# Fetching the next expert's weights, and the gates for a range check, in twelve paced pieces in a fused GateLoop and mixture-of-experts kernel

## The chip, the cores and the metric

The kernel runs on one core of a Trainium2 chip. The metric is the device time of one execution in microseconds (us), as the median of several runs; lower is better. The core has a matrix engine (TensorE; PE in the profile), whose results land in PSUM, a vector engine (DVE), an activation engine (ACT), a general engine (GpSimd; POOL), and a queue engine (SP) that here only starts transfers between the chip's memory (HBM) and the on-chip memory (SBUF).

## The reference

Two blocks follow each other. The first is a gated linear recurrence over 768 steps for 4 x 8 heads of 48 elements: a complex gate `a` is limited in magnitude, multiplies a 48 x 48 state, the outer product of key and value is added, and the query reads the state. Its result, seen as 3,072 rows of 384, goes through a mixture of eight experts in which each row goes to the one expert with the largest logit:

```python
    mag = np.sqrt(a_re * a_re + a_im * a_im)
    scale = np.minimum(mag, 0.999) / (mag + 1e-06)
    a_re_n, a_im_n = (a_re * scale, a_im * scale)
    for t in range(S):
        ...
        S_re, S_im = (new_re + kv, new_im)
        y[:, :, t] = np.einsum('bhd,bhde->bhe', q[:, :, t], S_re)
...
    logits = x @ w_gate
    expert_idx = np.argmax(logits, axis=1)
...
        h = np.maximum(x_sorted[lo:hi] @ w1[e], 0.0)
        y_sorted[lo:hi] = h @ w2[e]
    y = y_sorted[inv_perm]
    return (gate_w[:, None] * y).astype(np.float32)
```

Everything is float32. Each expert has `w1` (384 x 1024) and `w2` (1024 x 384), 1.5 MB each.

## The kernel before, in words

**The first block** fills the time up to about 270 us. It works through the sequence in 24 chunks of 128 rows, in an order written out by priorities, and writes its rows to a buffer `xd` in HBM. Since the rows' logits are ready only at its end, the eight experts are then sorted by how many rows they have, and each takes a **place**: place 0 is the fullest. Each place has a fixed capacity (`CAPS`: 448, 416, 416, 408, 400, 384, 376, 360 rows), so its instructions don't depend on the data; only the expert's number does. That number is in the tile `owner`, and SP reads it into a register (`load_w`, L588) to address the weights.

**A place** is done by `expert` (L676) in two layers, on tiles that two places use in turn: `wa` (`w1`), `wb` (`w2`), `xg` (gathered rows), `xt` (those rows turned so that the 384 inputs lie on partitions), and `ht` (the hidden layer). Even places use one set of these tiles, odd places the other.

- *Hidden layer*: for each of the 8 columns `f` of 128 hidden units, three matmuls (`hps`, two recorded passes each, so 6 records) go into one of four PSUM buffers, and a relu takes the result to `ht`: VectorE for even `f`, ScalarE for odd `f`.
- *Output layer*: for each tile of 128 rows, eight matmuls (`yps`, 16 records) sum over `f`, VectorE multiplies by the row's gate, and GpSimd scatters the rows into the result (`scatter`, L657). Two PSUM buffers take turns. Capacities that aren't a multiple of 128 leave a small last tile: in places 1 to 4 it has 32, 32, 24 and 16 rows. Its eight matmuls go to four column strips of the array, ScalarE copies three partial sums (`z`), and VectorE adds them.

While place i runs, GpSimd gathers the rows of place i+1 with one indirect transfer for each 32 rows, between its scatters, and VectorE turns them (`turn`, L628) once the hidden layer of place i is evicted. Place 0 is different: its first two row tiles are done in the first block's tail (`early`), and the others at the start of this part.

**The weights** of place i+2 are requested after place i: `wa` in four transfers of 32 partitions (384 KB each) and `wb` in one of 1.5 MB. Since place i+2 uses place i's tiles, `wa` starts when place i's hidden layer has read them, and `wb` when its output layer has.

**The range check** looks at every gate `a`, in six parts (`in_range`, L919), because the first block uses a form that holds only in a range. For part j it fetches two tiles `rc` of 128 x 1536 (768 KB each, real and imaginary part; two buffers), and VectorE makes two passes with a compare and a sum. `verdict` (L934) reads the sums, adds them over the partitions with a small matmul (`bp`), and gives a flag. If it is set, a slow exact path is run after the experts; with these inputs it isn't, and only the test of the flag and the last scatter follow.

**Order.** A scheduler sets the order on each engine from the dependencies and the program's order, and adds the semaphore waits. An engine's instructions wait in that order. SP's queue in this part holds only the transfers of `wa`, `wb` and `rc`; those of `rc` have no dependency but their buffers, so the first five are queued ahead of place 1's weights. `T["mm"]` always holds the last matmul that was written.

Of the kernel before, what the change touches and what calls it, by code (L numbers as in the profile page):

```python
# [10 lines left out]
FP = mybir.dt.float32  # L11
# [6 lines left out]
SYNC = mybir.DependencyInfo(mybir.DependencyClass.Sync, mybir.DependencyReason.DATA)  # L18
NOSYNC = mybir.DependencyInfo(mybir.DependencyClass.NoSync, mybir.DependencyReason.DATA)

P = 128
# [17 lines left out]
def kernel(  # L39
# [12 lines left out]
    nc = tc.nc  # L52
# [4 lines left out]
    E, _, F = w1.shape  # L57
    KD, KF = DM // P, F // P
# [7 lines left out]
    T = {}  # L66

    def mm(o, lhsT, rhs, start=True, stop=True):
        T["mm"] = nc.tensor.matmul(o, lhsT=lhsT, rhs=rhs, start=start, stop=stop, skip_group_check=True)  # L69
        return T["mm"]  # L70
# [12 lines left out]
    def iota(pattern, name, base=0, cm=0):  # L83
# [16 lines left out]
        out=last, in_=ones, pattern=[[0, P]], base=-(P - 1), channel_multiplier=1, compare_op=OP.is_ge, fill=0.0  # L100
# [484 lines left out]
    def tiles(i):  # L585
        return -(-CAPS[i] // P)

    def load_w(i, after=None):  # L588
        o = own0 if i == 0 else owner[:, i : i + 1]
        ev = nc.sync.value_load(o[0:1, 0:1], min_val=0, max_val=E - 1)  # L590
        wa = EP[i % 2].tile([P, KD, F], FP, tag="wa", name="wa")
        parts = [(slice(0, P), w1[ds(ev, 1)].rearrange("o (k p) f -> p (o k) f", p=P))]
        if i >= SQ:
            w = w1[ds(ev, 1)].rearrange("o (a k j) f -> a j (o k) f", a=4, k=KD)
            parts = [(slice(a * Q4, (a + 1) * Q4), w[a]) for a in range(4)]
        for p, w in parts:
            ins = nc.sync.dma_start(out=wa[p], in_=w)
            if after is not None:
                tc.add_manual_dep(ins.ins, after.ins.name, SYNC, reason="rows first")
        wb = EP[i % 2].tile([P, KF, DM], FP, tag="wb", name="wb")  # L600
        nc.sync.dma_start(out=wb, in_=w2[ds(ev, 1)].rearrange("o (i p) d -> p (o i) d", p=P))
        T["w", i] = wa, wb

    def gather(i, t0, t1, rows=N):

# [22 lines left out]
    def turn(i, t0, t1, ps, end=None):  # L628

        xg = T["xg", i]  # L630
        if t0 == 0:
            T["xt", i] = EP[i % 2].tile([P, KD, CAPS[0]], FP, tag="xt", name="xt")
        c0, c1 = t0 * P, min(CAPS[i], t1 * P)
        if i >= SQ:
            j1 = -(-c1 // Q4)
            T["turned"] = nc.vector.transpose(
                out=T["xt", i][:, :, c0 : j1 * Q4].rearrange("p k (j s) -> p j k s", s=Q4),
                in_=xg[:, c0 // Q4 * (DM // 4) : j1 * (DM // 4)].rearrange("p (j k x) -> p j k x", x=Q4, k=KD),
            )
            behind(T["turned"], [T["held"]])  # L640
            return
        for d in range(KD):
            tp = ps.tile([P, 512], FP, tag="tp", name="tp")
            for t in range(t0, t1):
                n = min(P, CAPS[i] - t * P)
                ins = nc.tensor.transpose(
                    out=tp[:, (t - t0) * P : (t - t0) * P + n],
                    in_=xg[0:n, t * DM + d * P : t * DM + (d + 1) * P],
                    identity=ident[0:n, 0:n],
                )  # L650
                if end is not None:
                    behind(ins, [end])
            T["turned"] = (nc.scalar.copy if d % 2 else nc.vector.tensor_copy)(
                out=T["xt", i][:, d, c0:c1], in_=tp[:, 0 : c1 - c0]
            )

    def scatter(y, n, i, t, to=None):  # L657
        ins = nc.gpsimd.indirect_dma_start(  # L658
            out=out,
            out_offset=bass.IndirectOffsetOnAxis(ap=row[0:n, i, t : t + 1] if to is None else to[0:n], axis=0),  # L660
            in_=y[0:n],
            in_offset=None,
            bounds_check=N - 1,
            oob_is_err=False,
        )
        if "drained" in T:
            behind(ins, [T["drained"]])
        T["scattered"] = T["scattered", i, t] = ins
# [4 lines left out]
        behind(ins, [T["scattered"]])  # L673
        T["drained"] = ins

    def expert(i, t0, t1, psH, psO, yp, between=None):  # L676

        xt = T["xt", i]
        wa, wb = T["w", i]
        if t0 == 0:  # L680
            T["ht", i] = EP[i % 2].tile([P, KF, CAPS[0]], FP, tag="ht", name="ht")
        ht = T["ht", i]
        c0, c1 = t0 * P, min(CAPS[i], t1 * P)
        for f in range(KF):
            ps = psH.tile([P, 512], FP, tag="tp" if psH is psT else "h", name="hps")[:, 0 : c1 - c0]
            for d in range(KD):
                mm(ps, wa[:, d, f * P : (f + 1) * P], xt[:, d, c0:c1], d == 0, d == KD - 1)
            if f % 2:
                nc.scalar.activation(out=ht[:, f, c0:c1], in_=ps, func=AF.Relu)  # L689
            else:  # L690
                T["held"] = ts(out=ht[:, f, c0:c1], in0=ps, scalar1=0.0, scalar2=None, op0=OP.max)  # L691
        for t in range(t0, t1):
            if t == t1 - 2 and between is not None:
                between()
            n = min(P, CAPS[i] - t * P)
            if psO is psA:
                ps = psO.tile([P, DM], FP, tag="at", padded_shape=[P, 512], name="yps")
            else:
                T["left"] = T.get("left", sum(tiles(j) for j in range(E)) - EARLY) - 1
                po = psO if T["left"] % 2 else EP["last"]  # L700
                ps = po.tile([P, DM], FP, tag="y", padded_shape=[P, 512], name="yps")
            g = gate[0:n, i, t : t + 1]
            y = yp.tile([P, DM], FP, tag="y", name="y", bufs=2 if psO is psA else 10)
            hs = ht[:, :, t * P : t * P + n]
            if n > 64:
                for f in range(KF):
                    mm(ps[0:n], hs[:, f], wb[:, f], f == 0, f == KF - 1)
                if i == E - 1 and t == t1 - 1:
                    T["last"] = ps[0:n], g
                    return  # L710
                ts(out=y[0:n], in0=ps[0:n], scalar1=g, scalar2=None, op0=OP.mult)  # L711
            else:

                w = 32 if n <= 32 else 64
                parts = P // w
                for f in range(KF):
                    j = f % parts
                    mm(ps[j * w : j * w + n], hs[:, f], wb[:, f], f < parts, f >= KF - parts)
                z = yp.tile([P, DM], FP, tag="z", name="z")
                for j in range(1, parts):  # L720
                    nc.scalar.copy(out=z[j * w : j * w + n], in_=ps[j * w : j * w + n])  # L721
                tt(out=y[0:n], in0=ps[0:n], in1=z[w : w + n], op=OP.add)  # L722
                for j in range(2, parts):
                    tt(out=y[0:n], in0=y[0:n], in1=z[j * w : j * w + n], op=OP.add)  # L724
                ts(out=y[0:n], in0=y[0:n], scalar1=g, scalar2=None, op0=OP.mult)
            scatter(y, n, i, t)

    def early(t0, t1, end):

# [47 lines left out]
    for hp in range(HP):  # L777
        for i in range(2):
            nc.sync.dma_start(
                out=back[i * 64 : i * 64 + D, hp, DD:], in_=w_gate[hp * DD + i * D : hp * DD + (i + 1) * D, :]  # L780
# [84 lines left out]
    for g in range(NT):  # L865
        u, b = divmod(g, B)
# [42 lines left out]
    yp = pool2("yp", 2, reuse_waits="tile")  # L909
# [5 lines left out]
    NR_ = 6  # L915
    RW = N * DM // P // NR_
    inr = const([P, 2 * NR_], "inr")

    def in_range(j):  # L919
        a = [rp.tile([P, RW], FP, tag=f"rc{i}", name=f"rc{i}") for i in range(2)]  # L920
        for t, src in zip(a, (a_re, a_im)):
            s = src.rearrange("b h t d -> (b h t d)").rearrange("(p f) -> p f", p=P)
            nc.sync.dma_start(out=t, in_=s[:, j * RW : (j + 1) * RW])
        junk = rp.tile([P, RW], FP, tag="junk", name="junk", bufs=1)
        for i, (op, sc) in enumerate(((OP.max, A_MIN), (OP.mult, -1.0))):
            stt(
                out=junk, in0=a[1], scalar=sc, in1=a[0], op0=op, op1=OP.is_lt,
                accum_out=inr[:, 2 * j + i : 2 * j + i + 1],
            )
# [22 lines left out]
    for i in range(E):  # L952
        t0 = EARLY if i == 0 else 0
        if i == E - 1:
            verdict()
        if i + 1 < E:
            gather(i + 1, 0, tiles(i + 1))
        expert(i, t0, tiles(i), psH, psO, yp, (lambda: turn(i + 1, 0, tiles(i + 1), psG)) if i + 1 < E else None)
        if i in DRAINS:
            drain()  # L960
        if i + 2 < E:
            load_w(i + 2)
        if 1 <= i <= NR_:
            in_range(i - 1)

# [3 lines left out]
    with tc.If(nc.values_load(flag[0:1, 1:2], min_val=0, max_val=P * (NC + 1)) > 0):  # L969
# [135 lines left out]
        n, a = 1, 0  # L1105
# [145 lines left out]
```

## Time and profile before

| | |
|---|---|
| median of 3 runs | 563.99 us (560.99 to 564.17) |
| profiled execution | 561.03 us, of which the span is 559.3 us |
| TensorE busy | 523.6 us, 94% of the span |
| VectorE, ScalarE, GpSimd busy | 289.6, 214.3, 132.7 us |
| transfers | 73.5 MB, 131 GB/s over the span |
| granted TensorE clock, mean | 0.991 |

The places stand in the profile as follows (start of the hidden layer and of the output layer on PE, us):

| place | rows | hidden | output |
|---|---|---|---|
| 0 (tiles 2 and 3) | 192 | 298.49 | 308.83 |
| 1 | 416 | 316.81 | 333.68 |
| 2 | 416 | 350.68 | 369.75 |
| 3 | 408 | 386.75 | 405.71 |
| 4 | 400 | 422.70 | 443.19 |
| 5 | 384 | 460.18 | 477.39 |
| 6 | 376 | 492.87 | 508.03 |
| 7 | 360 | 523.65 | 538.25 |

In a line of the timeline the first number is the start in us from the span's start, the second the time to the end of the last of the merged instructions, then engine, line, operation, output and inputs, the shape, and how often; the bracket is the engine's idle time before it and what ended it. A matmul's end is modelled, not measured. A row of windows gives the window, its length, the busy time of PE, its weight loads, DVE, ACT and POOL with the number of instructions, the granted clock as a share of full speed, the busy share of the 16 DMA engines, and GB/s. In the page's second part each digit is the busy share of a fortieth of the span, in tenths.

### The profile page before, as it was taken

Reading aid. Unit: us, or ns where it says so; the run is one execution under the profiler, and the core shown is the slowest. Engines: PE = TensorE matmul, PEld = TensorE weight load, DVE = VectorE, ACT = ScalarE, POOL = GpSimd, SP = SyncE. Lnnn points to the kernel's source line nnn. Section 1 sums busy time; section 2 is a strip of 40 time slices with the busy share of each in tenths; the row PEclk is TensorE's granted clock in tenths of the full one; section 3 lists DMA queues with packets and bytes.
Section 4 is the critical chain, followed back from the end, with each engine's and each line's share of the span. In section 5 each row is a group of like instructions: output and inputs, shape, how many; then the busy total and the mean of one; then the engine's idle time right before and its main releaser. Section 6 shows DMA issues by size and latency. Waiting matters only on the chain. (4 is left out here: it accounts for less than half of the span.)

```text
span 559.3 us, 8295 instructions
## 1 busy us (share of the span) xinstructions
PE 523.6 (94%) x3154; PEld 370.8 (66%) x3154; DVE 289.6 (52%) x585; ACT 214.3 (38%) x323; POOL 132.7 (24%) x161
## 2 busy tenths in 40 slices
PE   3889979999999999999998999899899899999996
PEld 3666858878888898888766555455454455555663
DVE  5378687788789888785565221251442412212210
ACT  6877988876588874553200010111101102000000
POOL 3000000000000000001058555707347064370101
PEclk9989989999999999999999999999999899999999
DMA  9977691938655826503468966753865444650001
GB/s 164 187 102 103 112 142 22 180 60 168 116 86 115 150 55 140 74 30 139 174 222 222 265 196 137 252 133 73 307 142 189 144 112 148 135 171 18 26 2 41
DMA packets 167735, 73.49 MB, mean 131 GB/s; under 512 B 149053, under 2 KB 160343, under 8 KB 167688
## 3 DMA queue, kind: packets, MB, share of 16 engines
q1 hardware_dynamic: 162792, 63.12, 52.4%
q0 software_dynamic: 4896, 9.77, 5.9%
q8 instruction: 27, 0.44, 0.3%
q14 instruction: 20, 0.16, 0.1%
HBM read 63.34 MB, written 9.73 MB: 131 GB/s over the span
## 5 line engine op out<-in xcount | busy, mean ns | idle before, releaser
L69 PE MATMUL hps<-xt,wa 128*128 128x416 f32 (+7 forms) x432 | 136.8, 472 | 8.8 <-issue 4.2
L69 PE MATMUL yps<-wb,ht 128*128 128x384 f32 (+6 forms) x464 | 134.1, 487 | 0.0
L69 PEld LDWEIGHTS hps<-xt,wa 128*128 128x128 f32 x432 | 79.9, 192 | 62.7 <-issue 32.0
L616 POOL DMA_INDIRECT xg<-xd,tok x92 | 94.8, 1030 | 88.5 <-PE tp L332 40.6
L69 PEld LDWEIGHTS yps<-wb,ht 128*128 128x128 f32 (+6 forms) x464 | 75.1, 175 | 55.8 <-issue 8.6
L689 ACT ACTIVATE ht<-hps 128x416 f32<-128x416 f32 (+7 forms) x36 | 16.7, 467 | 151.7 <-PE hps L69 103.9
L711 DVE TENSOR_SCALAR y<-yps,gate 128x384 f32<-128x384 f32 (+1 forms) x23 | 14.2, 618 | 93.2 <-PE yps L69 76.5
L658 POOL DMA_INDIRECT out_dram<-y,row x28 | 29.2, 1044 | 118.6 <-DVE y L711 100.9
L69 PE MATMUL at<-qt,kt 96*128 96x128 f32 x384 | 53.9, 280 | 0.7 <-DVE am L340 0.7
L691 DVE TENSOR_SCALAR ht<-hps 128x416 f32<-128x416 f32 (+7 forms) x36 | 18.8, 527 | 68.6 <-PE hps L69 41.8
L261 POOL DMA_DIRECT2D ai<-cd x4 | 3.4, 839 | 211.0 <-ACT R L175 100.6
L69 PEld LDWEIGHTS at<-qt,kt 96*128 96x128 f32 x384 | 47.7, 192 | 4.5 <-issue 1.1
L69 PE MATMUL yt<-am,v 128*48 128x128 f32 x384 | 42.7, 281 | 0.6 <-DVE am L340 0.6
L340 DVE TENSOR_TENSOR am<-at,tri 128x512 f32<-128x512 f32 x48 | 33.0, 688 | 18.6 <-PE at L69 18.5
L721 ACT COPY z<-yps 32x384 f32<-32x384 f32 (+3 forms) x13 | 6.1, 470 | 84.2 <-PE hps L69 58.0
L69 PE MATMUL yt<-qt,G 96*48 96x128 f32 x320 | 35.7, 274 | 0.0
L332 PE MATMUL tp<-ident,K 128*96 128x128 f32 x192 | 33.5, 284 | 1.3 <-DVE K L323 1.1
L69 PEld LDWEIGHTS dk<-v,K 128*96 128x96 f32 x320 | 32.9, 168 | 2.1 <-issue 1.0
L69 PE MATMUL dk<-v,K 128*96 128x48 f32 x320 | 33.5, 244 | 0.2 <-DVE G L371 0.2
L332 PE MATMUL tp<-ident,Q 128*96 128x128 f32 x192 | 33.4, 277 | 0.0
L334 ACT COPY kt<-tp 96x512 f32<-96x512 f32 x48 | 27.9, 581 | 11.0 <-PE tp L332 10.8
L334 ACT COPY qt<-tp 96x512 f32<-96x512 f32 x48 | 28.2, 587 | 4.2 <-PE tp L332 4.2
(170 smaller groups left out, 667.2 us busy)
## 6 DMA issues: line engine op xcount, KB each, us to landing
wb<-in_moe_w_dram SPq DMA_DIRECT2D x8, 1536.0 KB
wa<-in_moe_w_dram SPq DMA_DIRECT2D x28, 384.0 KB
q<-in_q_dram SPq DMA_DIRECT2D x12, 384.0 KB
k<-in_k_dram SPq DMA_DIRECT2D x12, 384.0 KB
v<-in_v_dram SPq DMA_DIRECT2D x12, 384.0 KB
xd<-x SPq DMA_DIRECT2D x24, 192.0 KB
rc<-in_a_re_dram SPq DMA_DIRECT2D x6, 768.0 KB
rc<-in_a_im_dram SPq DMA_DIRECT2D x6, 768.0 KB
```

Of the source, the lines that this page charges most:

```text
L69: T["mm"] = nc.tensor.matmul(o, lhsT=lhsT, rhs=rhs, start=start, stop=stop, skip_group_check=True)
L261: nc.gpsimd.dma_start(out=T["ai", u][0:1, b0:b1].rearrange("p b h d -> p (b h d)"), in_=cd[1, u - 1 : u, b0 * DM : b1 * DM], accum_op=OP.add,)
L332: nc.tensor.transpose(out=tp[0:DD, j], in_=X[:, hg * 4 + j], identity=ident)
L334: nc.scalar.copy(out=t[0:DD], in_=tp[0:DD])
L340: tt(out=am, in0=at, in1=bc(tri, 1, 4), op=OP.mult)
L616: ins = nc.gpsimd.indirect_dma_start(out=T["xg", i][0:n, j * w : (j + 1) * w], out_offset=None, in_=view, in_offset=bass.IndirectOffsetOnA ...
L658: ins = nc.gpsimd.indirect_dma_start(out=out, out_offset=bass.IndirectOffsetOnAxis(ap=row[0:n, i, t : t + 1] if to is None else to[0:n], a ...
L689: nc.scalar.activation(out=ht[:, f, c0:c1], in_=ps, func=AF.Relu)
L691: T["held"] = ts(out=ht[:, f, c0:c1], in0=ps, scalar1=0.0, scalar2=None, op0=OP.max)
L711: ts(out=y[0:n], in0=ps[0:n], scalar1=g, scalar2=None, op0=OP.mult)
L721: nc.scalar.copy(out=z[j * w : j * w + n], in_=ps[j * w : j * w + n])
```

## The change

For places 2 to 7 the weights are no longer requested after place i-2. `load_w` returns a list of eight jobs, four for `wa` (as they were cut before) and four for `wb` (two columns `f` each, 384 KB). `load_range` makes four more: each of the two `rc` tiles in two halves of 384 KB. During place i (1 to 6) the twelve jobs are for place i+1's weights and for part i-1 of the range check: first the four of `wa`, then `wb` and `rc` in turn. `begin` starts the next job and makes it wait for the matmul written last. It is called after every second hidden column, in the middle of every full output tile, and after every scatter; what is left then is started at the place's end. `in_range` no longer fetches; it runs after its place, as before. Weights of places 0 and 1 are fetched as before.

```diff
     def load_w(i, after=None):
...
-        for p, w in parts:
-            ins = nc.sync.dma_start(out=wa[p], in_=w)
-            if after is not None:
-                tc.add_manual_dep(ins.ins, after.ins.name, SYNC, reason="rows first")
+        jobs = [(wa[p], w) for p, w in parts]
         wb = EP[i % 2].tile([P, KF, DM], FP, tag="wb", name="wb")
-        nc.sync.dma_start(out=wb, in_=w2[ds(ev, 1)].rearrange("o (i p) d -> p (o i) d", p=P))
+        w = w2[ds(ev, 1)].rearrange("o (i p) d -> p (o i) d", p=P)
         T["w", i] = wa, wb
+        if i < 2:
+            for n, (o, src) in enumerate(jobs + [(wb, w)]):
+                ins = nc.sync.dma_start(out=o, in_=src)
+                if after is not None and n < len(jobs):
+                    tc.add_manual_dep(ins.ins, after.ins.name, SYNC, reason="rows first")
+            return []
+        return jobs + [(wb[:, f : f + 2], w[:, f : f + 2]) for f in range(0, KF, 2)]
+
+    def begin(jobs):
+
+        if jobs:
+            o, src = jobs.pop(0)
+            ins = nc.sync.dma_start(out=o, in_=src)
+            tc.add_manual_dep(ins.ins, T["mm"].ins.name, SYNC, reason="pace")
...
-    def expert(i, t0, t1, psH, psO, yp, between=None):
+    def expert(i, t0, t1, psH, psO, yp, between=None, jobs=()):
...
                 T["held"] = ts(out=ht[:, f, c0:c1], in0=ps, scalar1=0.0, scalar2=None, op0=OP.max)
+            if f % 2:
+                begin(jobs)
...
                     mm(ps[0:n], hs[:, f], wb[:, f], f == 0, f == KF - 1)
+                    if f == KF // 2:
+                        begin(jobs)
...
             scatter(y, n, i, t)
+            begin(jobs)
...
+    def load_range(j):
+
+        T["rc"] = [rp.tile([P, RW], FP, tag=f"rc{i}", name=f"rc{i}") for i in range(2)]
+        jobs = []
+        for t, src in zip(T["rc"], (a_re, a_im)):
+            s = src.rearrange("b h t d -> (b h t d)").rearrange("(p f) -> p f", p=P)[:, j * RW : (j + 1) * RW]
+            jobs += [(t[:, c : c + RW // 2], s[:, c : c + RW // 2]) for c in (0, RW // 2)]
+        return jobs
+
     def in_range(j):
-        a = [rp.tile([P, RW], FP, tag=f"rc{i}", name=f"rc{i}") for i in range(2)]
-        for t, src in zip(a, (a_re, a_im)):
-            s = src.rearrange("b h t d -> (b h t d)").rearrange("(p f) -> p f", p=P)
-            nc.sync.dma_start(out=t, in_=s[:, j * RW : (j + 1) * RW])
+        a = T["rc"]
...
-        expert(i, t0, tiles(i), psH, psO, yp, (lambda: turn(i + 1, 0, tiles(i + 1), psG)) if i + 1 < E else None)
+        jobs = []
+        if 1 <= i <= NR_:
+            w = load_w(i + 1)
+            jobs += w[:4]
+            for x in zip(w[4:], load_range(i - 1)):
+                jobs += x
+        expert(i, t0, tiles(i), psH, psO, yp, (lambda: turn(i + 1, 0, tiles(i + 1), psG)) if i + 1 < E else None, jobs)
+        while jobs:
+            begin(jobs)
         if i in DRAINS:
             drain()
-        if i + 2 < E:
-            load_w(i + 2)
         if 1 <= i <= NR_:
             in_range(i - 1)
```

## The prediction

> **What bounds the kernel now.** I read the page's busy shares first, then the chain of waits, then the timeline of each engine over places 0 to 7 (290 us to the end), because only there does the change move anything.
>
> ```profile
> PE 523.6 (94%) x3154; PEld 370.8 (66%) x3154; DVE 289.6 (52%) x585; ACT 214.3 (38%) x323; POOL 132.7 (24%) x161
> ...
> DMA  9977691938655826503468966753865444650001
> ...
> PE 30%; issue 4%; another core or an unknown queue 1%; DMA 1%; ACT 1%; DVE 0%; POOLq 0%; ACTq 0%
> ...
> L926 DVE SCALAR_TENSOR_TENSOR junk<-rc,rc x12: 1715/1748/1759, 292.3 to 443.2; 128x1536 f32<-128x1536 f32 x12
> ```
>
> TensorE is busy 94% of the span, and the chain in the second half is its two layers, `hps` and `yps`. Transfers run in half to two thirds of the time there, in bursts. The fourth line (from the answer on tile `rc`) prices a range check: two passes of 1.75 us and 0.08 us for each accumulator read, 3.66 us of VectorE.
>
> What the change could win is PE idle time. From 290 us on the PE timeline has eleven gaps: 0.79, 0.41, 0.47, 0.26, 0.90, then 0.49, 1.18, 1.37, 0.51, 2.31, 1.35; 10.04 us in all. But not all of them are idle time of the array. PE, SP and PE again:
>
> ```profile
> 349.60 1.15 PE L69 MATMUL yps<-wb,ht 128*32 128x384 f32 x12
> 350.68 8.65 PE L69 MATMUL hps<-xt,wa 128*128 128x416 f32 x24
> 359.82 2.36 PE L69 MATMUL hps<-xt,wa 128*128 128x416 f32 x6 [0.49 <-DVE ht L691]
> 363.36 6.55 PE L69 MATMUL hps<-xt,wa 128*128 128x416 f32 x18 [1.18 <-issue]
> 369.75 2.42 PE L69 MATMUL yps<-wb,ht 128*128 128x384 f32 x7
> ...
> 353.50 0.39 SPq L601 DMA_DIRECT2D wb<-in_moe_w_dram  x1
> ...
> 422.70 10.34 PE L69 MATMUL hps<-xt,wa 128*128 128x400 f32 x30
> 435.35 8.01 PE L69 MATMUL hps<-xt,wa 128*128 128x400 f32 x18 [2.31 <-ACT ht L689]
> ```
>
> The last matmul of place 1's 32-row tile is recorded as over by 350.75, yet the `wb` transfer that waits for it starts at 353.50: the array finishes that tile 2.8 us after the record. From 353.50 to 369.75 are 16.25 us for 48 hidden matmuls; the undisturbed 48 of place 1 took 16.87 (316.81 to 333.68). So the array did not stand still, and the gaps at 359 and 362 only ate the lead of the records. Place 3 the same: 389.55 to 405.71, 16.16 us, against 16.87 x 408/416 = 16.55. Place 5: 462.33 to 477.39, 15.06 against 15.57. Only place 4 lost: 426.20 to 443.19 is 16.99 against 16.22, and against place 3 scaled (16.16 x 400/408 = 15.84) it is 1.1 us. So at most about 1.1 us of the last six gaps is real.
>
> **The change part by part.**
>
> *The range rows leave place 0.* Before, SP issues five of the twelve range transfers between 283.9 and 296, beside the row gathers of place 0. The gather of its last rows is issued at 284.38, and PE waits for it until 291.72 (0.79 us), with 0.41 more at 292.87 for a copy that came late with it. With that traffic gone the rows are there at 290.66; VectorE still has the eviction of 290.86 ahead of the copy, so the last transpose moves from 292.87 to about 292.0. Gain 0.9 us (ends 0 and 1.2). The four VectorE passes in place 0 go too; the 0.26 and 0.90 at 303.7 and 305.8 follow late relus while `wa` of place 1 is already flowing, which stays. I take 0 there, ends 0 and a gain of 1.2.
>
> *The burst after each place goes.* Before, place i+2's `wa` starts when place i's hidden layer is over, and `wb` with two or three range halves (3 MB) at place i's end. After, one piece of 384 KB starts at every second hidden column, in the middle and at the end of every output tile. Place 4's stall of 2.31 us came under that burst, and the clock after it was low. The columns are busy time of PE, PEld, DVE, ACT, POOL, then granted clock, DMA share, GB/s:
>
> ```profile
> 354.00:356.00 2.00, 2.00 (x7) 1.06 (x6) 1.00 (x2) 0.93 (x2) 1.39 (x3) 1.00 0.61 131
> 356.00:358.00 2.00, 2.00 (x7) 1.14 (x6) 0.09 (x1) 0.00 (x0) 1.69 (x2) 1.00 1.03 367
> ...
> 408.00:410.00 2.00, 2.00 (x8) 1.21 (x7) 1.97 (x3) 0.00 (x0) 0.00 (x0) 1.00 1.07 215
> ...
> 436.00:438.00 2.00, 2.00 (x4) 0.92 (x3) 0.19 (x1) 0.00 (x0) 0.00 (x0) 0.55 0.38 151
> ```
>
> Ends: the whole 1.1 us gained, or as much lost if the new pattern delays a place likewise. Three of the four like places lost nothing, so I take the gain of 1.1.
>
> *Are the weights in time?* `wa`'s four pieces start in the hidden layer and have the output layer's 17 us to land; `wb`'s last starts at the place's end and is first needed late in the next output layer's first tile, 17 us later. **A rule speaks against the change**: the Trainium skill, "DMA: Bandwidth & Descriptors", section "Bandwidth", wants transfers of 1 MiB or more, and the section "Anatomy of one DMA" fits, for transfers that GpSimd issues, a fixed 2.0 us plus bytes/436e9. By it a piece of 393,216 bytes takes 2.9 us, twelve in a row 35 us: as long as a place (36 us), so the next would wait for weights. The row at 408 us shows four such pieces, already cut so before, keeping the engines at share 1.07 and 215 GB/s with no gap between: 1.8 us each, the fixed part beside the piece ahead; and pieces over 128 partitions run at 367 to 404 GB/s, 1 us each. By the rows a place's twelve take 4 x 1.8 + 8 x 1.0 = 15 us of 34. I follow the rows: cost 0. If pieces did run one by one, the last would be late by a few us in each place.
>
> *The new wait: a range check behind its own last piece.* The last piece of `rc` always starts at the place's last matmul (T0). In places 1 to 4 `wb`'s last and it follow T0, in places 5 and 6 the last three. In the order that the program builds, VectorE then has: relu of column 0 of the next place, two adds for the small tile, **both passes of the check**, relus of columns 2, 4, 6 (in places 6 and 7 one pass after each of relus 0 and 2). Who waits: relu 2 stands behind the check, and matmuls of column 6 need its PSUM buffer (four). Landing: issues take 0.40 and 0.58 us (SP rows at 353.5), data flow about 2 us after the issue (131 GB/s in the first window, 367 in the next), 0.79 MB at 395 GB/s take 2.0: T0 + 4.5; with three pieces, T0 + 5.5. Column 6 starts at T0 + 6 x 2.05 = 12.3; relu 2 takes 0.6 and the check 3.66, so it must start by T0 + 8.0. Even with relu 0 as late as now (395.97, T0 + 6.4, in place 3) and 1.6 us of relu and adds behind it, it starts at T0 + 8.0. I take 0.2 us in all; below nothing isn't possible, as this wait is new; the upper end is the slow rival.
>
> *The verdict moves.* Its matmul `bp` stood ahead of place 7's hidden layer; now it stands behind 17 of its 24, and waits for the last check: T0 + 5.5, pass 1.83, relu 0.53, pass 1.83, relu 0.53, compare 0.17 = T0 + 10.4. The array gets there at T0 + 17/24 x 14.6 = 10.3. No margin: 0.5 us, ends 0 and 2.
>
> *Signals and waits.* Matmuls signal 14 times more and PE waits 13 times more, twice in the middle of each first output tile. Rows of `yps`, which already carry four waits there, show 0.0 idle: cost 0; at 0.05 us each, 0.7. SP has nothing else queued in these places, so its waits hold up nobody; gathers, scatters and ScalarE keep their order.
>
> Sum: -0.9 - 1.1 + 0.2 + 0.5 = -1.3 us against the profiled execution's 561.03 (span 559.3), 559.7, or -0.23%. The median shown is 563.99, so 562.7.
>
> **Rivals.**
> 1. *The last range piece comes late* (slower). Place: VectorE at the start of places 2 to 7. It decides once the landing passes T0 + 8.0; each us beyond costs a us in places 2 to 5, and every us past T0 + 5.5 costs one at `bp`. At T0 + 9.0: 4 x 1.0 + 3.5 = 7.5, less the gain of 2.0: 566.5, median 569.5. For: the bursts of 3 MB begun at T0 now flow for 11 us (353.5 to 364.5), and relu 0 comes 3.6 to 6.4 us after T0 where 2.1 would do. Against: 0.79 to 1.18 MB stand there now, not 3.
> 2. *All eleven gaps are real, and even traffic closes them* (faster): 561.0 - 10.0 = 551.0, median 553.9. Against: the array's ends above.
> 3. *No effect*: place 0 keeps its wait, since `wa` and gathers still share the engines, and place 4 its own: +0.7 of new waits, 561.7, median 564.7.
>
> **How the numbers follow.** Forecast 0.57, rival 3 0.20, rival 1 0.18, rival 2 0.05. Within 1% (about what a measurement of this kernel can tell from no change) lie the forecast and rival 3, nearly all of it: 0.76; slower by over 1% is rival 1 with a little of the unknown: 0.19; faster by over 1% is rival 2 alone: 0.05. The range: down 1.2 for the gaps at 303 to 306 and 2 for the scatter of the runs, 559.5; up to rival 1, 569.5.
>
> **What would show it.** Right: no wait for `xg` at 291; the PE rows from 316 us on with fewer gaps; `rc` checks waiting for DMA on VectorE at the start of places 2 to 7, over by T0 + 12; `bp` inside place 7's hidden layer with a gap under 1 us; DMA share even at 0.4 to 0.7 over a place. Wrong: gaps before column 6 of places 2 to 5 that end with VectorE's `ht`, a first `yps` matmul that waits for `wb`, a gap before `bp` over 2 us, or place 0 with its old wait.

## The result, and the profile after

The changed kernel took 584.25 us (median of 4 runs, 572.1 to 589.0) where the kernel before took 563.89 beside it: **1.032 times as long** (95% interval 1.0246 to 1.0393). The ratio is the recorded one of the fast executions, and two of the changed kernel's four (at 589 us) were slow ones, so it is not the quotient of the two medians (1.036). The prediction had 562.7, no change. Further runs, told below, give a second half to this result: on another chip the same two kernels stood at **0.9995** (0.9974 to 1.0015), 547.32 us against 547.38. The profiled execution of the changed kernel took 589.0 us (span 587.3), the longest of its four, so the places add up to the upper end of the loss; a second one, with a span of 567.8 us, stands beside it below.

First the page of this execution, in the order in which the prediction showed the page before: busy shares, granted clock and DMA share in 40 slices, the chain that ended last, and the group of hidden matmuls with its busy time, mean and idle time before.

```profile
PE 532.6 (91%) x3154; PEld 377.2 (64%) x3154; DVE 289.0 (49%) x585; ACT 213.9 (36%) x323; POOL 137.1 (23%) x161
...
PEclk9999989999999999999976999799799898999999
DMA  9959583876558356043155236535455465476601
...
PE 78%; DVE 5%; ACT 4%; issue 4%; another core or an unknown queue 3%; DMA 2%; ACTq 1%; POOLq 0%; SPq 0%; DVEq 0%
...
L69 PE MATMUL hps<-xt,wa 128*128 128x416 f32 (+7 forms) x432 | 148.4, 504 | 28.0 <-DVE ht L703 14.9
```

Transfers are no longer in bursts, as the change intends. But the hidden matmuls have 28.0 us of idle time before them (8.8 before), more than half of it ended by VectorE's relu `ht`, and the clock is low in the slices behind the stalls. The PE timeline says where:

```profile
301.36 6.31 PE L69 MATMUL hps<-xt,wa 128*128 128x192 f32 x20 [5.41 <-issue]
314.91 2.29 PE L69 MATMUL hps<-xt,wa 128*128 128x192 f32 x6 [7.23 <-issue]
...
364.07 8.65 PE L69 MATMUL hps<-xt,wa 128*128 128x416 f32 x24
376.88 11.26 PE L69 MATMUL hps<-xt,wa 128*128 128x416 f32 x24 [4.16 <-DVE ht L703]
```

Place 0 stands for 5.41 and 7.23 us. Places 2 to 5 each stop after 24 records, which is four columns (the number of PSUM buffers), for 4.16, 4.32, 2.96 and 3.41 us. The hidden layers, from their first matmul to that of the output layer, in us:

| execution | place 0 | 1 | 2 | 3 | 4 | 5 |
|---|---|---|---|---|---|---|
| before, first profile (span 559.3) | 10.34 | 16.86 | 19.07 | 18.96 | 20.49 | 17.21 |
| after, first profile (587.3) | 27.19 | 16.86 | 23.90 | 23.77 | 21.15 | 20.70 |
| after, a second execution with the loss (567.8) | 15.35 | 16.87 | 19.68 | 21.89 | 20.30 | 18.01 |
| before, another chip (547.7) | 8.10 | 16.86 | 16.86 | 16.54 | 16.22 | 15.58 |
| after, that chip (544.9) | 8.09 | 16.86 | 16.86 | 16.54 | 16.22 | 15.58 |

Of the 28.0 us between the first two spans, 16.85 come in place 0 (less 3.46 by which it starts earlier, 2.71 of them from before anything that the change moves: the hidden layer ahead of it starts at 277.33 us in place of 280.04), 13.8 in places 2 to 5, and 0.9 in place 7; output layers differ by 0.1. The last two rows show that without the stalls both kernels take the same time to 0.01 us in every one of these layers, and that **the kernel before had stalls too**: 2.2 us in place 0 and 10.5 in places 2 to 5.

What does the array wait for? One stretch of the timeline of all engines, at the start of place 2 (`remote` stands where the profile finds no instruction that just ended behind the signal):

```profile
369.80 0.38 SPq L613 DMA_DIRECT2D wb<-in_moe_w_dram  x1
369.80 1.44 ACT L737 COPY z<-yps 32x384 f32<-32x384 f32 x3 [22.01 <-PE hps L69]
...
373.07 1.00 POOL L628 DMA_INDIRECT xg<-xd,tok  x1 [0.30 <-issue]
376.24 0.59 DVE L703 TENSOR_SCALAR ht<-hps 128x416 f32<-128x416 f32 x1 [3.84 <-remote]
```

The 32-row tile's last record ends at 364.14, but `z` and `wb`, which wait for its semaphore signal, start at 369.80. Column 0 of place 2 is recorded as over at 366.44, and its relu starts at 376.24. The trace's semaphore events have the signals of columns 0 to 3 at 376.21, 376.29, 376.37 and 376.44: four within 0.23 us, though the matmuls are 2.1 us apart. The matmuls were done and **their signals came up to 10 us late**, together. With four PSUM buffers unread, TensorE stands. That it really stands, the windows show (busy time of PE, PEld, DVE, ACT, POOL, then granted clock, DMA share, GB/s): the clock falls to half behind the gap.

```profile
374.00:376.00 2.00, 0.00 (x0) 0.00 (x0) 0.00 (x0) 0.00 (x0) 0.07 (x1) 0.84 0.23 57
376.00:378.00 2.00, 1.11 (x2) 0.76 (x3) 1.70 (x4) 0.93 (x2) 0.00 (x0) 0.50 0.35 61
```

Now the same place of the kernel before on the other chip: PE, then SP and ScalarE.

```profile
345.76 3.85 PE L69 MATMUL yps<-wb,ht 128*128 128x384 f32 x23
349.54 17.03 PE L69 MATMUL hps<-xt,wa 128*128 128x416 f32 x48
...
349.70 0.39 SPq L601 DMA_DIRECT2D wb<-in_moe_w_dram  x1
...
349.71 1.44 ACT L721 COPY z<-yps 32x384 f32<-32x384 f32 x3 [16.45 <-PE yps L69]
```

The 32-row tile's records end at 349.61, and `wb` and `z` start 0.1 us later. Forty-eight hidden matmuls follow without a gap. So the 2.8 us that the first profile shows between record and transfer are no time of the array.

In both first profiles the late signals lie beside rows of GpSimd's gathers, one each 1.3 us without a pause, and at places 2 to 5 the last of them comes 2 to 4 us after the last gather is over. The trace lacks some signals, so the lateness is counted by pairing signals and records in order. Of the 268 that pair up before 280 us in the first profile of the kernel before, none is over 0.03 us late.

### The profile page after: what moved, and what is told of

Same layout as the page of the kernel before. It is cut to its first block, busy times and chain, and to the rows that moved or that the text cites. A ratio compares the mean times of both kernels' runs of the same rounds, so it can differ in the third digit from the quotient of the medians.

```text
span 587.3 us, 8426 instructions
## 1 busy us (share of the span) xinstructions
PE 532.6 (91%) x3154; PEld 377.2 (64%) x3154; DVE 289.0 (49%) x585; ACT 213.9 (36%) x323; POOL 137.1 (23%) x161
## 4 chain that ended last, share of the span: by engine, by line
PE 78%; DVE 5%; ACT 4%; issue 4%; another core or an unknown queue 3%; DMA 2%; ACTq 1%; POOLq 0%; SPq 0%; DVEq 0%
PE yps L69 22%; PE hps L69 21%; PE yt L69 7%; PE tp L332 7%; PE at L69 7%; PE dk L69 4%; PE cst L69 3%; PE xb L69 3%; PE csl L69 2%; PE sp L69 1%; DMA rc<-in_a_im_dram 1%; DMA xd<-x 1%; ACT z L737 1%; DVE junk L949 1%
## 5 line engine op out<-in xcount | busy, mean ns | idle before, releaser
L69 PE MATMUL hps<-xt,wa 128*128 128x416 f32 (+7 forms) x432 | 148.4, 504 | 28.0 <-DVE ht L703 14.9
L69 PEld LDWEIGHTS hps<-xt,wa 128*128 128x128 f32 x432 | 88.4, 211 | 84.8 <-issue 42.0
L670 POOL DMA_INDIRECT out_dram<-y,row x28 | 33.1, 1183 | 144.9 <-DVE y L727 125.1
L332 PE MATMUL tp<-ident,Q 128*96 128x128 f32 x192 | 33.4, 277 | 0.0
```

Of the source, the lines that this page charges most:

```text
L332: nc.tensor.transpose(out=tp[0:DD, j], in_=X[:, hg * 4 + j], identity=ident)
L670: ins = nc.gpsimd.indirect_dma_start(out=out, out_offset=bass.IndirectOffsetOnAxis(ap=row[0:n, i, t : t + 1] if to is None else to[0:n], a ...
```

## The experiments

The runs came in eight groups, each on another chip. The time of the kernel before, run beside each, tells them apart: 547.3 to 548.6 us on five, 553.5 to 555.5 on three. Every trace from the five has its signals on time (at most 0.07 us late), every trace from the three has late ones, the latest of each 7.5 to 14.8 us (2.5 in `f6_before_spread`, which spreads the gathers). I call them *punctual* and *late*. The first measurement (563.99) was a late one. Why they differ is not known. Each chip was met in one group only, and the late groups also hold fewer executions (two to four of each changed or edited kernel, against 12 to 20), so that the chip and what else went with the group can't be told apart.

**First group: halves, no waits, spaced gathers.** Theories: G, a long row of gathers on GpSimd makes TensorE's signals late; P, the paced pieces do; T, traffic beside the gathers relieves them. `e1_spaced`, on the changed kernel (`more` begins the next gathers behind the instruction that it is given):

```diff
                 T["held"] = ts(out=ht[:, f, c0:c1], in0=ps, scalar1=0.0, scalar2=None, op0=OP.max)
+                more(T["held"], 2)
...
-                ts(out=y[0:n], in0=ps[0:n], scalar1=g, scalar2=None, op0=OP.mult)
+                more(ts(out=y[0:n], in0=ps[0:n], scalar1=g, scalar2=None, op0=OP.mult), 3)
...
-        if i + 1 < E:
-            gather(i + 1, 0, tiles(i + 1))
+        if i == 0:
+            list(gather(1, 0, tiles(1)))
+        T["next"] = gather(i + 2, 0, tiles(i + 2)) if i + 2 < E else iter(())
```

> The changed kernel, with GpSimd's gathers for place i+2 begun in twos and threes behind place i's own relus and evictions (from place 0 on), instead of thirteen in one row over the boundary between two places. Theory G (a long unbroken row of gathers on GpSimd holds TensorE's semaphore signals back): the stalls of 3 to 4.3 us after place 2 to 5's fourth group of columns, and the half clock behind them, go: 584 less about 15 and less about 8, so 560 to 566; only place 0, where the gathers of places 0 and 1 still follow each other, keeps part of its 13. Rival P (the paced pieces themselves do it, by waiting on TensorE or by what they leave undone at a place's end): the stalls stay, 580 to 586.

`e2_nopace`:

```diff
             ins = nc.sync.dma_start(out=o, in_=src)
-            tc.add_manual_dep(ins.ins, T["mm"].ins.name, SYNC, reason="pace")
```

> The changed kernel with the dependence of each piece on the product ahead of it left out: the same twelve pieces in the same order on SP's queue, each gated by its buffer alone. Rival P: TensorE's signals come as before the change, 562 to 568. Theory G alone, with the gathers where they are: the stalls at the boundaries stay, 580 to 586. If what relieves the signals is other traffic beside the gathers (theory T), the pieces begin as soon as their buffers allow, which puts traffic at the boundary and into place 0 again: 566 to 574.

`e3_weights` takes `in_range` from the kernel before, with its fetches, and keeps the weights' pieces:

```diff
-            jobs += w[:4]
-            for x in zip(w[4:], load_range(i - 1)):
-                jobs += x
+            jobs += w
```

> Weights in paced pieces as in the changed kernel, the range fetches and their checks as in the kernel before (whole, unpaced). If place 0's loss of 13 us is from the range rows having left it (their transfers or their passes on VectorE broke up the gathers there), it comes back: about 571, with the boundaries of places 2 to 5 as in the changed kernel. If the weights' pieces have nothing to do with the boundaries, 562 to 566. If the range rows have nothing to do with it: 582 to 586.

`e4_range` is the kernel before with only the range rows given to `begin`, after every scatter:

```diff
+        jobs = load_range(i - 1) if 1 <= i <= NR_ else []
...
+        while jobs:
+            begin(jobs)
```

> The other half: weights as in the kernel before, only the range rows fetched in four pieces behind a place's products. If the range rows alone carry place 0's loss: 564 plus 13, 575 to 579, with boundaries as before. If they carry the boundaries too: 582 to 588. If neither: 563 to 566.

Measured: 548.42 (ratio 1.0016, 0.9996 to 1.0035), 547.23 (0.9986, 0.9966 to 1.0005), 547.5 (1.0004, 0.9985 to 1.0022) and 546.55 (0.9974, 0.9958 to 0.9990), where the kernel before took 547.65. No expectation was met, since none had thought of a punctual chip. Only the last moved: 0.26% or 1.4 us faster, the order of the 0.9 us that the prediction had for the range rows leaving place 0.

**Second group: the two kernels themselves**, unedited.

> The changed kernel itself once more, beside fresh runs of the kernel before: in the four runs ahead of this one (two in which one half of the change is undone, one without the waits, one with the gathers spaced) all stood within 0.3% of the kernel before at 547.65, and none of their traces has a TensorE signal over 1 us late. Theory C (the loss needs signals that come late on their own account, which these executions did not have): the changed kernel is then within 0.5% of before too, 545 to 551 where before takes 547 to 548, and about 3% over it only where before itself takes about 564. Rival W (the loss needs both halves of the change together, whatever the signals): about 3% over before here too, 562 to 566.

> The kernel before, for its trace beside the changed kernel's on the same chip. Theory C: where its time is near 547, the gaps in TensorE's rows behind the 32-row tiles (1.18, 1.37 and 2.31 us in the first profile) and the late signals behind them are gone, and the whole difference of 14 to 16 us from the first profile lies in places 0 to 6. If the signals are as late as in the first profile (up to 10 us) and the time is 547 all the same, they cost nothing, and the theory falls.

Measured: the changed kernel 547.32, ratio 0.9995 (0.9974 to 1.0015); the kernel before 549.39 in its one profiled execution. Theory C (the loss needs signals that come late on their own account) holds, and W (the two halves of the change together bring it, whatever the signals) falls. The groups of hidden matmuls on the two pages, before and after:

```profile
L69 PE MATMUL hps<-xt,wa 128*128 128x416 f32 (+7 forms) x432 | 132.9, 466 | 0.0
```

```profile
L69 PE MATMUL hps<-xt,wa 128*128 128x416 f32 (+7 forms) x432 | 133.1, 466 | 0.0
```

No idle time, and 466 ns a matmul where the first profiles have 472 and 504: idle time and half clock come and go together.

**Third group: what a late signal costs.** Both kernels, with the first relu on either engine held until the next place's last gather has landed:

```diff
+            if f < 2 and 2 <= i <= 5:
+                tc.add_manual_dep(ins.ins, T["rows", i + 1].ins.name, SYNC, reason="hold")
```

> The changed kernel with the first relu on VectorE and the first on ScalarE of places 2 to 5 made to wait for the last gather of the next place's rows, which is about where the first profile has TensorE's signals of these columns arrive (376.21, some 3 us after the last gather began at 373.07). Theory C prices the late signals by themselves: a gap in TensorE's rows of some 3 to 4 us in each of the four places, and up to 2 us of half clock after each, so 12 to 23 us over the kernel before, 560 to 570 where that takes 547. If a stall of this kind is absorbed later in the place: under 4 us over it.

> The same hold put into the kernel before. Theory C: the late signals cost whichever kernel has them about the same, so within 4 us of the held changed kernel. Rival W (the paced pieces make a stall dearer, since each waits for a product that comes later, and the weights behind it with it): the held changed kernel is over 6 us slower than this one.

> The changed kernel once more, beside fresh runs of the kernel before. Theory C: within 0.7% of it where its time is near 547; 2 to 4% over it where its time is near 564 and its trace has late signals of TensorE beside GpSimd's gathers.

This chip was late: before 553.5, the plain changed kernel 570.14 (two executions), ratio 1.0313 (1.0271 to 1.0356). So **the loss of 3% repeats on a late chip**. Held, the changed kernel took 579.96 (1.0466, 1.0409 to 1.0524) and the kernel before 582.29 (1.0544, 1.0490 to 1.0599). The holds cost more than I had put them at, and that the two totals are so close is luck: the changed kernel took 8.7 us more in place 0 and 9.0 less in places 2 to 5, where its holds ended sooner. The stall in place 2, changed kernel and kernel before:

```profile
370.55 11.55 PE L69 MATMUL hps<-xt,wa 128*128 128x416 f32 x24 [3.94 <-DVE ht L704]
```

```profile
364.45 11.35 PE L69 MATMUL hps<-xt,wa 128*128 128x416 f32 x24 [6.45 <-DVE ht L692]
```

In places 2 to 5 the hidden layers took 24.4 and 33.4 us over their undisturbed times, of which 14.1 and 22.6 us are the idle time itself. The rest, slowed matmuls behind the gaps, is 10.3 and 10.8 us, alike in both. So what the record has against W in its second form, that the pieces make a stall dearer, is this: beyond its own length a stall costs both kernels the same. And the held kernel before, with late signals, took 8.10 us in place 0, where the changed kernel took 15.35 and, held, 16.81.

**Fourth group: the halves again**, unchanged, and the kernel before. Theory R: place 0 loses because the range rows left it.

> Weights in paced pieces, the range rows fetched and checked as in the kernel before, again, for an execution with late signals (where before takes over 550). There the changed kernel lost 7.3 us in place 0 and 14.6 in places 2 to 5, while the held kernel before lost nothing in place 0. Theory R (place 0's loss comes with the range rows that left it): place 0's columns take 8.3 us again and the kernel loses at the boundaries alone, 1 to 2% over before. If the weights' pieces alone carry all of the loss: 3% over it. Where before takes 547: within 0.3%, as the first time.

> Only the range rows paced, the weights as before, again. Theory R, with late signals: place 0's columns take 15 to 17 us in place of 8.3, the boundaries lose what they lose in the kernel before: 1.3 to 2.3% over before. If the range rows carry nothing: the same as before within 0.5%. Where before takes 547: 0.1 to 0.4% under it, as the first time.

> The changed kernel with GpSimd's gathers begun in twos and threes behind the place's own relus and evictions, again. Theory G, with late signals: they are late only inside a long unbroken row of gathers, so the gaps in places 2 to 5 go and the kernel loses in place 0 alone (where two places' gathers still follow each other): 1 to 2% over before, or under it by up to 1% if the kernel before loses at its boundaries too. If the gathers have no part in it: 3% over before. Where before takes 547: within 0.3%.

> The kernel before, for its trace on the same chip. With late signals: place 0's columns in 8.3 us, and gaps of 1 to 3 us in all in places 1 to 5, so that the difference to the changed kernel's 22 us of loss can be put down place by place. Without: no gap in any place.

A punctual chip: 548.62 (1.0020, 1.0001 to 1.0040), 547.27 (1.0001, 0.9972 to 1.0030) and 548.2 (1.0015, 0.9992 to 1.0038), with 547.28 before, and no gap in the places of the profiled kernel before. They tell nothing of late signals, and do not confirm the 0.26% of the first group. So the next kernels held both kinds of place in one execution.

**Fifth group: spaced and unspaced rows of gathers in one kernel**, on `e3_weights`:

```diff
-            if i >= 2:
+            if i in SPACED:
+                yield ins
+            elif i >= 2:
                 behind(ins, [T["scattered", i - 2, 3 * m // len(parts)]])
...
+    SPACED = (3, 5)
```

> Weights in paced pieces, range rows as in the kernel before, and the gathers for places 3 and 5 alone spaced out over the places two ahead of them, so that one execution holds both kinds: no row of gathers lies over the starts of places 2 and 4, and one lies over those of places 3 and 5. With late signals, theory G: places 2 and 4 take their columns in 17.0 and 16.4 us without a gap, places 3 and 5 lose 2 to 6 us each; if the gathers have no part in it, all four lose. Theory R: place 0's columns take 8.3 us. Where before takes 547 there are no gaps anywhere and the time is within 0.4% of it.

A late chip (before 555.49); two runs of 558.05 and 568.53 us. The PE timeline of the first, places 0, 2, 3, 4 and 5:

```profile
295.66 8.26 PE L69 MATMUL hps<-xt,wa 128*128 128x192 f32 x48
...
352.56 17.03 PE L69 MATMUL hps<-xt,wa 128*128 128x416 f32 x48
...
386.42 8.49 PE L69 MATMUL hps<-xt,wa 128*128 128x408 f32 x24
397.67 8.74 PE L69 MATMUL hps<-xt,wa 128*128 128x408 f32 x24 [2.76 <-issue]
...
423.24 16.39 PE L69 MATMUL hps<-xt,wa 128*128 128x400 f32 x48
...
456.45 8.01 PE L69 MATMUL hps<-xt,wa 128*128 128x384 f32 x24
464.95 2.20 PE L69 MATMUL hps<-xt,wa 128*128 128x384 f32 x6 [0.49 <-DVE ht L707]
468.50 6.07 PE L69 MATMUL hps<-xt,wa 128*128 128x384 f32 x18 [1.35 <-issue]
```

Theory G is met: places 2 and 4, with no row of gathers over their starts, ran 48 matmuls without a gap; places 3 and 5, with a row, lost 3.3 and 2.4 us. The gathers that left place 2's start went to place 1, where those of two places now followed each other from 312 to 349 us. Its output layer took 23.95 us in place of 17.00, but that is no late signal's doing. VectorE turns the next place's rows ahead of the output tiles' evictions, and waited for those rows:

```profile
341.56 1.48 DVE L652 STREAM_TRANSPOSE xt<-xg 128x1248 f32<-128x1248 f32 x1 [14.26 <-DMA xg<-xd,tok]
```

The signals of place 1's hidden layer, beside this same row, were on time. So a long row does not always make them late. Theory R is met as well: place 0 lost nothing. GpSimd and VectorE in place 0:

```profile
289.29 1.00 POOL L628 DMA_INDIRECT xg<-xd,tok  x1 [0.30 <-issue]
289.48 1.75 DVE L955 SCALAR_TENSOR_TENSOR junk<-rc,rc 128x1536 f32<-128x1536 f32 x1
290.60 1.51 POOL L628 DMA_INDIRECT xg<-xd,tok  x1 [0.30 <-issue]
...
291.27 1.76 DVE L955 SCALAR_TENSOR_TENSOR junk<-rc,rc 128x1536 f32<-128x1536 f32 x1
292.41 1.50 POOL L628 DMA_INDIRECT xg<-xd,tok  x1 [0.30 <-issue]
```

A gather beside a range pass takes 1.50 us in place of 1.00; the next two passes stretch gathers to 2.17 and 1.64, and each of the four ends 0.9 us behind its pass. The Trainium skill, "SBUF — State Buffer", section "SBUF: two separate sides", says why such a meeting can be: VectorE, reading two tensors from SBUF, and a GpSimd instruction that reads SBUF share a pair of ports, which the one that starts first holds to its end. So with the range rows there, GpSimd's row in place 0 is held up four times; without them it runs on at 1.3 us a gather. That these holds, and not the rows' transfers, keep the signals in time is argued only: no run has one without the other. Against it stands place 3 of this run, where two passes fell beside the row and signals were still 8.6 us late.

**Sixth group: the other half mixed, and an attempt to win.** `f7_range_mixed` puts the same spacing on `e4_range`. `f6_before_spread` is the kernel before with every place's gathers spread over a whole place, two behind each eviction and each of VectorE's relus:

```diff
+                more(i + 1, T["held"])
...
+                more(i + 2, ts(out=y[0:n], in0=ps[0:n], scalar1=g, scalar2=None, op0=OP.mult))
```

> The other half of the change alone (range rows in four pieces behind a place's products, weights as in the kernel before), with the gathers for places 3 and 5 alone spaced. Theory R, with late signals: with the range rows gone from place 0, its columns take 15 to 17 us (8.3 with them, in the kernel with the weights alone paced). If place 0 takes 8.3 us here too, the loss there needs the weights' pieces, which in place 0 differ in nothing but the second place's. Theory G: places 2 and 4 without a gap, places 3 and 5 with.

> The kernel before, unchanged in its weights and range rows, with each place's thirteen gathers spread over a whole place's time: two behind each of the three full tiles' evictions two places ahead, then two behind each of VectorE's relus of the place ahead. Theory G, with late signals (before over 550): no unbroken row of over six gathers is left from place 1 on, so signals are on time, the columns of places 2 to 5 take 17.0, 16.7, 16.4 and 15.8 us, and the kernel runs 1 to 2% under before, at 546 to 549. If the gathers are not what makes the signals late: within 0.5% of before. Where before takes 547: within 0.4%, nothing to win.

A late chip (before 553.64). `f7_range_mixed` took 576.17 (two executions), ratio 1.0416 (1.0347 to 1.0486). Its PE timeline, place 0, then the stall of place 3:

```profile
300.80 5.20 PE L69 MATMUL hps<-xt,wa 128*128 128x192 f32 x20 [2.00 <-DVE xt L664]
306.43 1.24 PE L69 MATMUL hps<-xt,wa 128*128 128x192 f32 x6 [0.43 <-DVE ht L702]
309.27 3.19 PE L69 MATMUL hps<-xt,wa 128*128 128x192 f32 x18 [1.59 <-ACT ht L700]
...
412.54 10.97 PE L69 MATMUL hps<-xt,wa 128*128 128x408 f32 x24 [6.67 <-DVE ht L702]
```

Without the range rows, and with the weights as before, place 0 took 14.42 us: theory R from the other side. Places 2 and 4 lost nothing again, places 3 and 5 lost 9.4 and 2.1, and place 1, under two places' gathers, 9.4. Here the loss did go where the row went: in place 1 a relu's signal came 11 us late and later ones up to 14.8.

`f6_before_spread` took 579.32, ratio 1.0465 (1.0411 to 1.0519). It did what it was for: the hidden layers of places 1 to 5 took 16.86, 16.86, 16.55, 16.22 and 15.58, all undisturbed on a late chip, with no signal over 2.5 us late. But output layers of places 1 to 4 took 24.6 to 27.8 us in place of 17.0:

```profile
383.58 1.48 DVE L636 STREAM_TRANSPOSE xt<-xg 128x1248 f32<-128x1248 f32 x1 [11.61 <-DMA xg<-xd,tok]
...
388.43 1.14 DVE L713 TENSOR_SCALAR y<-yps,gate 128x384 f32<-128x384 f32 x2
...
389.10 8.88 PE L69 MATMUL yps<-wb,ht 128*128 128x384 f32 x32 [5.34 <-DVE y L713]
```

The transposition of the next place's rows stands ahead of the evictions on VectorE. Its last gather, issued at 374.63, landed only at 383.3, behind the four transfers of `wa`. This loss, read in place 2, is of my own making and no late signal's.

**Seventh group: the same with the transposition behind the place's second eviction.**

```diff
-            behind(T["turned"], [T["held"]])
+            behind(T["turned"], [T["held"]] + ([T["freed"]] if i >= 2 else []))
```

> The kernel before with the gathers spread as in the run ahead, and VectorE's transposition of the next place's rows ordered behind the second eviction of the place (in the run ahead it stood in front of the first, waited up to 9 us for gathers that landed beside the weights, and cost 5 to 8 us in each place's output tiles). With late signals (before over 550): columns of places 2 to 5 in 17.0, 16.7, 16.4 and 15.8 us as there, output tiles in 17.1 us or up to 2 us over it, and the whole 0.5 to 1.5% under before, 546 to 551. If the spread gathers make the signals of the output tiles late, whose two buffers bear less: 1 to 3% over before. Where before takes 547: within 0.4%.

A punctual chip: 552.12, ratio 1.0027 (0.9996 to 1.0058). Place 2 waited 3.1 us for its transposed rows and ran its columns in 18.56 us behind that wait; nothing else was lost. Whether it wins on a late chip was not seen.

**Eighth group: the weights' half a third time.**

> Weights alone in paced pieces, for the third time, for an execution with late signals (before over 550). Place 0's columns take 8.3 us (theory R). If the weights' pieces make the boundaries dearer too, as the first pair of profiles has it (places 2 to 5 lost about 10.5 us before the change and 22 after), 1 to 2% over before; if the whole loss is the range rows', within 0.7% of before. Where before takes 547: within 0.3%, as twice.

Punctual again: 548.99, ratio 1.0015 (0.9996 to 1.0034). The split at the boundaries stays open. No version here beat both kernels.

## Why the prediction was wrong, point by point

**The failed step is the reading of the gaps**: "the array finishes that tile 2.8 us after the record ... the gaps at 359 and 362 only ate the lead of the records ... at most about 1.1 us of the last six gaps is real". With signals on time the transfer starts 0.1 us after the record, so the record was right and the signal late. All six gaps in places 2 to 5 were real (7.2 us), and with the slowed matmuls behind them these hidden layers lost 10.5 us. A sum that takes the signals for on time has no term for what makes them later, and the loss came in just that. I had the late signal before my eyes and took it for slow arithmetic, because I measured the time from the late signal to the next layer and found it short.

**The range rows leave place 0**, put at a gain of 0.9 us. The term was mis-sized and had the wrong sign. Its reckoning of the wait for `xg` was good: from the start of the hidden layer ahead to its own first column place 0 took 17.70 us in place of 18.45, a gain of 0.75. But its columns then took 16.85 us longer, and the four VectorE passes that leave with the rows, or the rows' transfers, had been put at 0. Across the late executions place 0's columns took 8.1 to 10.3 us with the range rows in it (four traces) and 14.4 to 27.2 without (four traces). On punctual chips the step was right: that first stretch took 17.59 us in all six traces without the range rows there and 18.1 to 20.3 in the six with them. The whole did not move measurably, since place 7 took 0.9 us back (below).

**The burst goes, place 4 gains 1.1**: wrong. Place 4's stall of 2.31 us ended with late signals and not with the burst; after the change it stood 2.96 us. On a punctual chip there is no stall to win, with the burst or without. That places 2 to 5 lost 13.8 us more after the change is measured; in its second late trace the changed kernel lost 14.7 us there in all (places 2 to 5: 19.68, 21.89, 20.30 and 18.01), some 4 more than the kernel before in the first profile. That part of the extra is the change's can only be estimated from the times: on that chip the kernel before stood about 6 us over its punctual time in all (553.5 against 547.5), and the changed kernel lost 14.7 us in these places alone. How much of it is the change's, by what step, and which half carries it stays open.

**Weights in time at no cost**: right. No `yps` matmul waited for `wb` in any of the six traces of the two kernels; the pieces' rows, not the rule of 1 MiB, gave the right answer. **Signals and waits at no cost**: right where signals are on time, 0.00 to 0.01 us in each layer.

**The new wait**: 0.2 predicted. On a punctual chip all six checks waited for their rows as forecast, 14.3 us in all, and held up no column of places 2 to 6. In the first profile only the checks in places 6 and 7 waited for their rows, 7.6 us in two waits; the gaps that "end with VectorE's `ht`" stand before column 4, not column 6, and before any pass of the check had begun (377.78, relu 0 at 376.24). So rival 1, whose time of 569.5 was the nearest, is not what happened. **The verdict**: 0.5 predicted; the gap before `bp` is 0.50 us, and place 7's columns took 0.9 us longer, since `bp` itself now stands among them.

Rival 2 had the premise right (the gaps are real) and the conclusion wrong (even traffic closes them). Rival 3, no effect, is the result on a punctual chip. None had a signal that comes late as its mechanism, and that the time came nearest to rival 1's would have been luck.

## What to carry to other kernels

When something that waits for an engine starts well after the engine's record ends, don't add the difference to the engine's work: look whether several such signals arrive together, and whether the clock falls; here both meant that the engine was done and stood. Keep GpSimd's indirect transfers in short groups or away from stretches where two or four PSUM buffers are all the slack, and before moving work away from beside them ask what it was holding up. And a single measurement on a single chip can hold a loss that another chip does not have: run the pair again elsewhere before explaining a few per cent.

## What was not expected of the hardware

- TensorE's semaphore signals came up to 14.8 us late in some groups of runs, several about 0.08 us apart, and only during or just after rows of nine or more of GpSimd's indirect transfers (1.3 us each, hardly a pause); not every such row brought them, and why they come is not known. The transfers themselves are as fast as elsewhere: packets of 3072 bytes on GpSimd's queue took 0.13 us in the median on a late and on a punctual chip alike.
- A gap of 4.16 us brought half clock, 0.84 in its window and 0.50 in the next, and the 24 matmuls behind it took 11.26 us where the 24 ahead of it took 8.65. One of 2.96 us in place 4 did the same: 10.02 us against 8.33. The length alone does not decide: behind a gap of 2.11 us in place 4 of `e9_after_third` they took 10.02 us as well, behind the 2.76 us in place 3 of `f5_weights_mixed` only 8.74 against 8.49, at a clock of 1.00.
- A range pass on VectorE stretched a gather on GpSimd from 1.00 to between 1.50 and 2.17 us.
